# A decode step of attention plus a gated feed-forward: feed-forward moved behind head 0, and the output projection done by groups of heads

## Chip, cores and metric

One core of one Trainium2 chip. The metric is the device time of the slowest (here the only) core in microseconds (us), lower is better. The kernel before took 2587.42 us, the median of four runs (2586.26 to 2589.1). A single profile shows one execution; its span is about 1.8 us shorter than the time of that run.

## The reference

One token attends to a cache of 65536 positions with 32 heads. A feed-forward of the same token is mixed in by a scalar gate.

```python
# x (1,1,512) bf16; k_cache, v_cache (1,32,65536,128) bf16; wq (512,4096); wo (4096,512)
# w_gate, w_up (512,1792); w_down (1792,512); gate_w (512)
g = sigmoid((x * gate_w).sum(-1, keepdims=True))
q = (x @ wq) split into 32 heads of 128
p = softmax(q @ k_cache^T * 128 ** -0.5)
a = concat_heads(p @ v_cache) @ wo
b = (silu(x @ w_gate) * (x @ w_up)) @ w_down
out = g * a + (1 - g) * b
```

The two caches are 1074 MB together. Everything else that is read is about 16 MB.

## The kernel before

The DMA engines copy from the chip's memory (HBM) into its on-chip memory (SBUF); a transfer is asked for by an engine and stands in that engine's queue. K is read in tiles of 4 MB (two buffers) on SyncE's queue, V in tiles of 2 MB (three buffers) on ScalarE's. VectorE multiplies K by a broadcast q and folds the 128 products down to one score. ScalarE takes the exponential. TensorE multiplies V by the probabilities. Four chunks of 4096 positions make a segment (one K tile, two V tiles), and four segments a head.

```python
# ... q for all heads first: wq (4 MB) on nc.sync, 32 matmuls, 8 copies
with tc.tile_pool(name="ffn_w", bufs=1) as wpool:       # takes the room of wq, so it waits for q
    wg_sb = wpool.tile([P, KT, F], bf16, name="wg_sb");  nc.scalar.dma_start(out=wg_sb, in_=awg)
    wu_sb = wpool.tile([P, KT, F], bf16, name="wu_sb");  nc.sync.dma_start(out=wu_sb, in_=awu)
    # ... 112 small matmuls -> gu_ps, silu on VectorE, w_down on nc.scalar, 14 matmuls -> b_sb
wo_sb = _load_wo()                                        # nc.sync, takes the room of ffn_w
# ...
O_ps = psum_o.tile([P, H], f32, name="O_ps")
for h in range(H):
    for sgi, seg_chunks in enumerate(seg_plans[h]):
        for ci, c in enumerate(seg_chunks):
            # ... every 4th chunk: nc.sync.dma_start(out=K_big, in_=A_k_cache[...])
            nc.vector.tensor_tensor(out=prod, in0=K_t, in1=q_rep, op=ALU.mult)
            # ... four halving adds and a tensor_reduce -> S_sb
        nc.scalar.activation(out=P_sb, in_=S_sb, func=ACT.Exp, scale=scale, accum_out=rowsum[...])
        for ci, c in enumerate(seg_chunks):
            # ... every 2nd chunk: nc.scalar.dma_start(out=V_big, in_=A_v_cache[...])
            # ... 32 matmuls into O_ps[:, h : h + 1]
tot_ps = psum_tot.tile([P, H * NSEGMAX], f32, name="tot_ps")
nc.tensor.matmul(tot_ps, lhsT=ones, rhs=rowsum, start=True, stop=True)
tot_sb = consts.tile([P, H * NSEGMAX], f32, name="tot_sb")   # these three live among the constants
# ... tot_h = consts.tile([P, H]); recip = consts.tile([P, H]); oT = O_ps * recip
for h in range(H):
    nc.tensor.matmul(a_ps, lhsT=oT[:, h : h + 1], rhs=wo_sb[:, h, :], start=(h == 0), stop=(h == H - 1))
# ... out = (a - b) * g + b
```

The softmax here doesn't subtract the row's maximum and nothing guards it: scores larger than these inputs give would overflow.

Of the kernel before, what the change touches and what calls it, by code (L numbers as in the profile page):

```python
# [7 lines left out]
ACT = mybir.ActivationFunctionType  # L8
ALU = mybir.AluOpType
AXIS = mybir.AxisListType  # L10
P = 128
# [3 lines left out]
PROD_BUFS = 2  # L15
WMAX = 4096
CHUNKS_PER_SEG = 4
POOL_MULT_EVERY = 0
VQ = "scalar"
LAST_HEAD_SPLIT = 1  # L20
PROD_INPLACE = 0
DMA_MULT = 4
VDMA_MULT = 2
WQ_STAGED = 0
WO_LATE = 1
FFN_STAGED = 0
WO_ENG = "sync"
# [3 lines left out]
def kernel(  # L31
# [14 lines left out]
    nc = tc.nc  # L46
    bf16 = mybir.dt.bfloat16
    f32 = mybir.dt.float32

    _, H, Sk, Dh = A_k_cache.shape  # L50
    D = A_x.shape[2]
# [16 lines left out]

    consts = ctx.enter_context(tc.tile_pool(name="consts", bufs=1))
    psum_o = ctx.enter_context(tc.tile_pool(name="psum_o", bufs=1, space=bass.MemoryType.PSUM))  # L70
# [4 lines left out]

# [8 lines left out]
    gval = consts.tile([1, 1], f32, name="gval")  # L84

# [4 lines left out]
    def _load_wo():  # L90
        wo_pool = ctx.enter_context(tc.tile_pool(name="wo_pool", bufs=1))
        wo_sb = wo_pool.tile([P, H, D], bf16, name="wo_sb")
        {"gpsimd": nc.gpsimd, "sync": nc.sync, "scalar": nc.scalar}[WO_ENG].dma_start(
            out=wo_sb, in_=A_wo.rearrange("(h p) n -> p h n", p=P)
        )
        return wo_sb

    wo_sb = None
    if not WO_LATE:
        wo_sb = _load_wo()  # L100
# [3 lines left out]
    prodpool = None if PROD_INPLACE else ctx.enter_context(tc.tile_pool(name="prod", bufs=PROD_BUFS))  # L104
# [3 lines left out]
    awq = A_wq.rearrange("(t p) f -> p t f", p=P)  # L108
    with tc.tile_pool(name="wq_pool", bufs=(2 if WQ_STAGED else 1)) as wq_pool:
        if not WQ_STAGED:  # L110
            wq_sb = wq_pool.tile([P, KT, H * Dh], bf16, name="wq_sb")
            nc.sync.dma_start(out=wq_sb, in_=awq)
        for g in range(H // HG):
            if WQ_STAGED:
                wq_g = wq_pool.tile([P, KT, HG * Dh], bf16, name="wq_g")
                nc.sync.dma_start(out=wq_g, in_=awq[:, :, g * HG * Dh : (g + 1) * HG * Dh])
                w_rhs = lambda t: wq_g[:, t, :]
            else:
                w_rhs = lambda t: wq_sb[:, t, g * HG * Dh : (g + 1) * HG * Dh]
            qg_ps = psum_misc.tile([P, HG * Dh], f32, name="qg_ps", tag="misc")  # L120
            for t in range(KT):
                nc.tensor.matmul(  # L122
                    qg_ps,
                    lhsT=X_bc[:, t, :],
                    rhs=w_rhs(t),
                    start=(t == 0),
                    stop=(t == KT - 1),
                )
            nc.scalar.activation(  # L129
                out=q_bc_sb[:, g * HG * Dh : (g + 1) * HG * Dh], in_=qg_ps, func=ACT.Copy  # L130
            )

    awg = B_w_gate.rearrange("(t p) f -> p t f", p=P)
    awu = B_w_up.rearrange("(t p) f -> p t f", p=P)
    awd = B_w_down.rearrange("(t p) n -> p t n", p=P)
    GB = 4
    with tc.tile_pool(name="ffn_w", bufs=(2 if FFN_STAGED else 1)) as wpool:
        gu_ps = psum_misc.tile([P, 2 * FT], f32, name="gu_ps", tag="misc")
        if FFN_STAGED:
            for fb in range(0, FT, GB):  # L140
                nb = min(GB, FT - fb)
                for wi, aw in enumerate((awg, awu)):
                    w_b = wpool.tile([P, KT, GB * P], bf16, name="wgu_b")
                    nc.scalar.dma_start(
                        out=w_b[:, :, : nb * P], in_=aw[:, :, fb * P : (fb + nb) * P]
                    )
                    for fi in range(nb):
                        ft = fb + fi
                        for t in range(KT):
                            nc.tensor.matmul(  # L150
                                gu_ps[:, wi * FT + ft : wi * FT + ft + 1],
                                lhsT=w_b[:, t, fi * P : (fi + 1) * P],
                                rhs=xT[:, t : t + 1],
                                start=(t == 0),
                                stop=(t == KT - 1),
                            )
        else:
            wg_sb = wpool.tile([P, KT, F], bf16, name="wg_sb")
            nc.scalar.dma_start(out=wg_sb, in_=awg)
            wu_sb = wpool.tile([P, KT, F], bf16, name="wu_sb")  # L160
            nc.sync.dma_start(out=wu_sb, in_=awu)
# [10 lines left out]
        gu_sb = consts.tile([P, 2 * FT], f32, name="gu_sb")  # L172
        nc.vector.tensor_copy(out=gu_sb, in_=gu_ps)  # L173
        eg = consts.tile([P, FT], f32, name="eg")
        nc.scalar.activation(out=eg, in_=gu_sb[:, :FT], func=ACT.Exp, scale=-1.0)
        nc.vector.tensor_scalar_add(eg, eg, 1.0)
        nc.vector.reciprocal(eg, eg)
        hprod = consts.tile([P, FT], f32, name="hprod")
        nc.vector.tensor_tensor(out=hprod, in0=gu_sb[:, :FT], in1=eg, op=ALU.mult)
        hT = consts.tile([P, FT], bf16, name="hT")  # L180
        nc.vector.tensor_tensor(out=hT, in0=hprod, in1=gu_sb[:, FT:], op=ALU.mult)  # L181
        b_ps = psum_misc.tile([1, D], f32, name="b_ps", tag="misc")
        if not FFN_STAGED:
            wd_sb = wpool.tile([P, FT, D], bf16, name="wd_sb")
            nc.scalar.dma_start(out=wd_sb, in_=awd)
        for ft in range(FT):
            if FFN_STAGED:
                wd_b = wpool.tile([P, D], bf16, name="wd_b")
                nc.scalar.dma_start(out=wd_b, in_=awd[:, ft, :])
            else:  # L190
                wd_b = wd_sb[:, ft, :]
            nc.tensor.matmul(  # L192
                b_ps,
                lhsT=hT[:, ft : ft + 1],
                rhs=wd_b,
                start=(ft == 0),
                stop=(ft == FT - 1),
            )
        nc.vector.tensor_copy(out=b_sb, in_=b_ps)  # L199

        xg = consts.tile([1, D], f32, name="xg")
        s_t = consts.tile([1, 1], f32, name="s_t")
        nc.vector.tensor_tensor_reduce(
            out=xg, in0=x_row, in1=gw_row, scale=1.0, scalar=0.0,
            op0=ALU.mult, op1=ALU.add, accum_out=s_t,
        )
        eg2 = consts.tile([1, 1], f32, name="eg2")
        nc.scalar.activation(out=eg2, in_=s_t, func=ACT.Exp, scale=-1.0)
        nc.vector.tensor_scalar_add(eg2, eg2, 1.0)
        nc.vector.reciprocal(gval, eg2)  # L210

    if WO_LATE:
        wo_sb = _load_wo()
# [18 lines left out]
    O_ps = psum_o.tile([P, H], f32, name="O_ps")  # L232
    a_ps = psum_a.tile([1, D], f32, name="a_ps")
    oT = consts.tile([P, H], bf16, name="oT")

    chunk_counter = 0
    for h in range(H):
        qb = q_bc_sb[:, h * Dh : (h + 1) * Dh]
# [6 lines left out]
        for sgi, seg_chunks in enumerate(plan):  # L245
            segcols = len(seg_chunks) * J
            S_sb = spool.tile([P, SEGCOLS], f32, name="S_sb")
            for ci, c in enumerate(seg_chunks):
# [10 lines left out]
                prod = K_t if PROD_INPLACE else prodpool.tile([P, J, Dh], bf16, name="prod")  # L259
                mult_eng = nc.vector  # L260
                if POOL_MULT_EVERY and (chunk_counter % POOL_MULT_EVERY) == (POOL_MULT_EVERY - 1):
                    mult_eng = nc.gpsimd
                chunk_counter += 1
                mult_eng.tensor_tensor(out=prod, in0=K_t, in1=q_rep, op=ALU.mult)  # L264
# [15 lines left out]
            )  # L280
            for ci, c in enumerate(seg_chunks):
                m = c % VDMA_MULT
                if m == 0:
                    V_big = vpool.tile([P, VDMA_MULT * J, Dh], bf16, name="V_big")
                    veng = {"scalar": nc.scalar, "sync": nc.sync, "gpsimd": nc.gpsimd}[VQ] if VQ != "mix" else (nc.scalar if c % 2 == 0 else nc.gpsimd)
                    veng.dma_start(
# [6 lines left out]
                for j in range(J):  # L293
# [3 lines left out]
                        O_ps[:, h : h + 1],  # L297
# [4 lines left out]
                    )  # L302

    tot_ps = psum_tot.tile([P, H * NSEGMAX], f32, name="tot_ps")
    nc.tensor.matmul(tot_ps, lhsT=ones, rhs=rowsum, start=True, stop=True)  # L305
    tot_sb = consts.tile([P, H * NSEGMAX], f32, name="tot_sb")
    nc.vector.tensor_copy(out=tot_sb, in_=tot_ps)  # L307
    tot_h = consts.tile([P, H], f32, name="tot_h")
    if NSEGMAX > 1:
        nc.vector.tensor_reduce(  # L310
            out=tot_h, in_=tot_sb.rearrange("p (h s) -> p h s", s=NSEGMAX), axis=AXIS.X,
            op=ALU.add,
        )
    else:
        nc.vector.tensor_copy(out=tot_h, in_=tot_sb)
    recip = consts.tile([P, H], f32, name="recip")
    nc.vector.reciprocal(out=recip, in_=tot_h)
    nc.vector.tensor_tensor(out=oT, in0=O_ps, in1=recip, op=ALU.mult)  # L318

    for h in range(H):  # L320
        nc.tensor.matmul(  # L321
            a_ps,
            lhsT=oT[:, h : h + 1],
            rhs=wo_sb[:, h, :],
            start=(h == 0),
            stop=(h == H - 1),
        )
# [39 lines left out]
```

## Time and profile before

| what | value | where it is read |
|---|---|---|
| span of the profiled run | 2587.3 us (its time was 2589.1) | head of the page |
| DMA rate in the middle | 427 GB/s at a share of 1.00 to 1.01 | busy time by stretch |
| VectorE busy | 2471 us, 96% | page, part 1 |
| transfers nearly dry | 60 to 70 us | busy time by stretch |
| from the end of the last V product to the end of the span | 14.5 us | timeline |

The first fence is from the page of the kernel before: the span, the busy times, the DMA share in 40 slices (in tenths), the rate in each slice, and the chain of work that ended last.

```profile
span 2587.3 us, 37728 instructions
...
PE 500.9 (19%) x16576; PEld 468.0 (18%) x16576; DVE 2471.0 (96%) x3093; ACT 58.9 (2%) x273; POOL 0.4 (0%) x5
...
DMA  9999999999999999999999999999999999999996
GB/s 377 377 423 429 429 429 428 428 429 430 428 427 427 429 422 430 429 424 426 431 426 428 425 428 425 432 427 424 429 425 427 426 429 427 424 430 425 426 426 289
...
DMA V_big<-in_A_v_cache_dram 73%; DVE prod L268 8%; DVE prod L264 8%; PE O_ps L296 5%; DMA K_big<-in_A_k_cache_dram 1%; DVE S_sb L272 1%; DMA wq_sb<-in_A_wq_dram 1%; DMA wg_sb<-in_B_w_gate_dram 1%; PE qg_ps L122 0%; PE a_ps L321 0%; PE gu_ps L165 0%; PE tot_ps L305 0%; DVE out_sb L332 0%; DVE diff L330 0%; DVE b_sb L199 0%
```

The DMA engines are full from end to end; only the first two slices and the last are slow. The Trainium skill, "DMA: Bandwidth & Descriptors", Specifications, gives 435 GB/s as the ceiling of the fabric; the middle of this trace sits 2% below it. The next fence is the view of busy time by stretch of the same kernel. In each row come the length of the stretch, busy us and instruction count of each engine, then TensorE's clock, DMA share and GB/s.

```profile
core 0: us, PE busy (x) PEld busy (x) DVE busy (x) ACT busy (x) POOL busy (x), PEclk, DMA share, GB/s
...
60.00:65.00 5.00, 2.43 (x92) 2.35 (x88) 2.53 (x8) 0.22 (x1) 0.00 (x0) 0.50 0.67 211
65.00:70.00 5.00, 0.00 (x0) 0.00 (x0) 5.00 (x5) 0.00 (x0) 0.00 (x0) 0.50 0.15 39
...
1100.00:1600.00 500.00, 95.19 (x3264) 91.01 (x3264) 492.05 (x613) 10.46 (x52) 0.00 (x0) 0.50 1.01 427
1600.00:2100.00 500.00, 95.17 (x3264) 91.00 (x3264) 490.00 (x612) 10.06 (x50) 0.00 (x0) 0.50 1.00 427
```

The timeline of the same kernel says why they ran dry. Its columns are start, length, engine and line, and in brackets the idle time before with what ended it.

```profile
36.99 0.37 SPq L161 DMA_DIRECT2D wu_sb<-in_B_w_up_dram  x1
...
37.40 31.82 SPq L252 DMA_DIRECT2D K_big<-in_A_k_cache_dram  x2
...
43.62 3.56 DVE L268 TENSOR_TENSOR prod<-prod 128x2048 bf16<-128x2048 bf16 x4
...
62.47 0.19 DVE L173 COPY gu_sb<-gu_ps 128x28 f32<-128x28 f32 x1 [15.29 <-PE gu_ps L165]
...
2570.94 1.87 PE L296 MATMUL O_ps<-P_sb,V_big 128*128 128x1 bf16 x64 [2.99 <-DMA V_big<-in_A_v_cache_dram]
2572.64 0.50 PEld L305 LDWEIGHTS tot_ps<-rowsum,ones 128*128 128x128 f32 x2
2572.66 1.09 PE L305 MATMUL tot_ps<-rowsum,ones 128*128 128x224 f32 x2
...
2575.28 8.38 PE L321 MATMUL a_ps<-wo_sb,oT 128*1 128x512 bf16 x32 [1.52 <-DVE oT L318]
...
2585.18 0.26 SPq L336 DMA_DIRECT2D out_dram<-out_sb  x1
```

VectorE stopped for 15.3 us in the middle of the first K tile, because its copy of the feed-forward product stands there in its order. The third K tile could not be asked for until VectorE was done with the first (the second of the two K issues on that line ends at 69 us). At the end, 32 projection matmuls of 8.4 us stand between the last V product and the output.

### The profile page before, as it was taken

What the parts mean: (1) busy time and instruction counts of PE and PEld (TensorE: products, weight loads), DVE (VectorE), ACT (ScalarE), POOL (GpSimd) and SP (SyncE); (2) the same over time, 40 slices, a digit from 0 to 9 for tenths busy, and PEclk for the clock granted to TensorE, in tenths of its full rate; (3) what the DMA queues carried; (4) which work ended last, traced back from release to release, by engine and by line L of the source; (5) the groups of instructions that cost most, each with busy time, mean ns of one, the idle gap of its engine ahead of it and who ended that gap; (6) DMA issues with size and microseconds to landing.
All of it is one profiled execution on the core that took longest, in us unless ns stands there. A gap on an engine that the chain in (4) does not pass through costs nothing.

```text
span 2587.3 us, 37728 instructions
## 1 busy us (share of the span) xinstructions
PE 500.9 (19%) x16576; PEld 468.0 (18%) x16576; DVE 2471.0 (96%) x3093; ACT 58.9 (2%) x273; POOL 0.4 (0%) x5
## 2 busy tenths in 40 slices
PE   1211211211111212111212211121221112122113
PEld 1111211111111111111111111111111111111112
DVE  1899999999999999999999999999999999999996
ACT  1000000000000000000000000000000000000000
POOL 0000000000000000000000000000000000000000
PEclk8555555555555555555555555555555555555555
DMA  9999999999999999999999999999999999999996
GB/s 377 377 423 429 429 429 428 428 429 430 428 427 427 429 422 430 429 424 426 431 426 428 425 428 425 432 427 424 429 425 427 426 429 427 424 430 425 426 426 289
DMA packets 63498, 1090.06 MB, mean 421 GB/s; under 512 B 6755, under 2 KB 12646, under 8 KB 13670
## 3 DMA queue, kind: packets, MB, share of 16 engines
q1 hardware_dynamic: 24134, 547.11, 49.7%
q10 hardware_dynamic: 39200, 540.56, 49.3%
q8 instruction: 129, 2.11, 0.3%
q14 instruction: 35, 0.29, 0.0%
HBM read 1087.64 MB, written 0.00 MB: 420 GB/s over the span
## 4 chain that ended last, share of the span: by engine, by line
DMA 76%; DVE 17%; PE 6%; issue 0%; SPq 0%; ACT 0%; DVEq 0%; ACTq 0%
DMA V_big<-in_A_v_cache_dram 73%; DVE prod L268 8%; DVE prod L264 8%; PE O_ps L296 5%; DMA K_big<-in_A_k_cache_dram 1%; DVE S_sb L272 1%; DMA wq_sb<-in_A_wq_dram 1%; DMA wg_sb<-in_B_w_gate_dram 1%; PE qg_ps L122 0%; PE a_ps L321 0%; PE gu_ps L165 0%; PE tot_ps L305 0%; DVE out_sb L332 0%; DVE diff L330 0%; DVE b_sb L199 0%
## 5 line engine op out<-in xcount | busy, mean ns | idle before, releaser
L264 DVE TENSOR_TENSOR prod<-K_big,q_bc_sb 128x4096 bf16<-128x4096 bf16 x512 | 1148.4, 2284 | 67.3 <-DMA K_big<-in_A_k_cache_dram 66.5
L268 DVE TENSOR_TENSOR prod<-prod 128x2048 bf16<-128x2048 bf16 (+3 forms) x2048 | 1186.0, 651 | 0.0
L296 PE MATMUL O_ps<-P_sb,V_big 128*128 128x1 bf16 x16384 | 474.4, 165 | 2021.6 <-DMA V_big<-in_A_v_cache_dram 1667.4
L296 PEld LDWEIGHTS <-V_big 128*128 128x128 bf16 x16384 | 456.6, 104 | 2039.7 <-DMA V_big<-in_A_v_cache_dram 1796.3
L272 DVE TENSOR_REDUCE S_sb<-prod 128x32 f32<-128x256 bf16 x512 | 188.9, 410 | 0.5 <-DVE prod L268 0.5
L277 ACT ACTIVATE P_sb<-S_sb 128x128 bf16<-128x128 f32 (+1 forms) x131 | 40.2, 307 | 2452.2 <-PE O_ps L296 1527.2
L277 ACT ACTIVATION_READ_ACCUMULATOR P_sb<-S_sb 128x1 f32 x131 | 24.4, 186 | 0.0
L173 DVE COPY gu_sb<-gu_ps 128x28 f32<-128x28 f32 x1 | 0.2, 187 | 15.3 <-PE gu_ps L165 15.3
L122 PE MATMUL qg_ps<-wq_sb,X_bc 128*128 128x512 bf16 x32 | 8.7, 441 | 28.2 <-DMA wq_sb<-in_A_wq_dram 28.2
L307 DVE COPY tot_sb<-tot_ps 128x224 f32<-128x224 f32 x1 | 0.4, 392 | 12.9 <-PE tot_ps L305 12.9
L122 PEld LDWEIGHTS <-X_bc 128*128 128x128 bf16 x32 | 3.5, 110 | 33.0 <-issue 20.7
L330 DVE TENSOR_TENSOR diff<-a_ps,b_sb 1x512 f32<-1x512 f32 x1 | 0.7, 679 | 8.5 <-PE a_ps L321 8.5
L321 PE MATMUL a_ps<-wo_sb,oT 128*1 128x512 bf16 x32 | 8.4, 428 | 1.5 <-DVE oT L318 1.5
L88 DVE COPY X_bc<-xT 128x128 bf16<-128x128 bf16 x4 | 0.6, 220 | 8.3 <-DMA xT<-in_A_x_dram 8.3
L165 PE MATMUL gu_ps<-xT,wg_sb 128*128 128x1 bf16 x56 | 3.0, 165 | 22.3 <-DMA wg_sb<-in_B_w_gate_dram 22.3
L192 PE MATMUL b_ps<-wd_sb,hT 128*1 128x512 bf16 x14 | 5.4, 568 | 9.0 <-DVE hT L181 9.0
L165 PEld LDWEIGHTS <-wg_sb 128*128 128x128 bf16 x56 | 2.6, 104 | 22.8 <-issue 22.8
L129 ACT ACTIVATE q_bc_sb<-qg_ps 128x512 bf16<-128x512 f32 x8 | 4.8, 597 | 21.9 <-PE qg_ps L122 21.9
L321 PEld LDWEIGHTS <-oT 128*1 128x1 bf16 x32 | 2.9, 92 | 7.1 <-DVE oT L318 2.1
L192 PEld LDWEIGHTS <-hT 128*1 128x1 bf16 x14 | 1.5, 114 | 12.5 <-DVE hT L181 9.1
L165 PE MATMUL gu_ps<-xT,wu_sb 128*128 128x1 bf16 x56 | 3.0, 165 | 0.0
L165 PEld LDWEIGHTS <-wu_sb 128*128 128x128 bf16 x56 | 2.6, 104 | 0.0
(24 smaller groups left out, 8.3 us busy)
## 6 DMA issues: line engine op xcount, KB each, us to landing
V_big<-in_A_v_cache_dram ACTq DMA_DIRECT2D x256, 2048.0 KB, 25.5
K_big<-in_A_k_cache_dram SPq DMA_DIRECT2D x128, 4096.0 KB, 19.8
wq_sb<-in_A_wq_dram SPq DMA_DIRECT2D x1, 4096.0 KB, 26.3
wo_sb<-in_A_wo_dram SPq DMA_DIRECT2D x1, 4096.0 KB, 37.1
wu_sb<-in_B_w_up_dram SPq DMA_DIRECT2D x1, 1792.0 KB
wg_sb<-in_B_w_gate_dram ACTq DMA_DIRECT2D x1, 1792.0 KB, 22.1
wd_sb<-in_B_w_down_dram ACTq DMA_DIRECT2D x1, 1792.0 KB
xT<-in_A_x_dram SPq DMA_DIRECT2D x1, 1.0 KB, 8.7
```

The costliest lines, as they stand in the source:

```text
L88: nc.vector.tensor_copy(out=X_bc[:, t, :], in_=xT[:, t : t + 1].to_broadcast([P, P]))
L122: nc.tensor.matmul(qg_ps, lhsT=X_bc[:, t, :], rhs=w_rhs(t), start=(t == 0), stop=(t == KT - 1),)
L129: nc.scalar.activation(out=q_bc_sb[:, g * HG * Dh : (g + 1) * HG * Dh], in_=qg_ps, func=ACT.Copy)
L165: nc.tensor.matmul(gu_ps[:, wi * FT + ft : wi * FT + ft + 1], lhsT=wsb[:, t, ft * P : (ft + 1) * P], rhs=xT[:, t : t + 1], start=(t == 0), ...
L192: nc.tensor.matmul(b_ps, lhsT=hT[:, ft : ft + 1], rhs=wd_b, start=(ft == 0), stop=(ft == FT - 1),)
L264: mult_eng.tensor_tensor(out=prod, in0=K_t, in1=q_rep, op=ALU.mult)
L268: nc.vector.tensor_tensor(out=prod[:, :, 0:half], in0=prod[:, :, 0:half], in1=prod[:, :, half : 2 * half], op=ALU.add,)
L272: nc.vector.tensor_reduce(out=S_sb[:, ci * J : (ci + 1) * J], in_=prod[:, :, 0:8], axis=AXIS.X, op=ALU.add,)
L277: nc.scalar.activation(out=P_sb[:, :segcols], in_=S_sb[:, :segcols], func=ACT.Exp, scale=scale, accum_out=rowsum[:, h * NSEGMAX + sgi : h ...
L296: nc.tensor.matmul(O_ps[:, h : h + 1], lhsT=V_t[:, j, :], rhs=P_sb[:, col : col + 1], start=(gcol == 0), stop=(gcol == NB - 1),)
L321: nc.tensor.matmul(a_ps, lhsT=oT[:, h : h + 1], rhs=wo_sb[:, h, :], start=(h == 0), stop=(h == H - 1),)
L330: nc.vector.tensor_tensor(out=diff, in0=a_ps, in1=b_sb, op=ALU.subtract)
```

## The change

Two things are intended. The feed-forward and wo are put behind head 0 in program order, with wo on GpSimd's queue, so that K and V stream from the start. The normalisation and projection of finished heads are done inside the stream, in groups of 8, 8, 8 and 7 heads, so that only head 31 is left for the end. Selectors that were always off are removed as well.

```diff
-WO_ENG = "sync"
+WO_ENG = "gpsimd"
+FFN_POS = 0
...
-    psum_o = ctx.enter_context(tc.tile_pool(name="psum_o", bufs=1, space=bass.MemoryType.PSUM))
+    psum_o = ctx.enter_context(tc.tile_pool(name="psum_o", bufs=2, space=bass.MemoryType.PSUM))
...   (feed-forward and wo load become functions; w_down is now asked for with the other two)
+    groups = [list(range(g, min(g + 8, H - 1))) for g in range(0, H - 1, 8)] + [[H - 1]]
+    def _project(heads, O_g):
+        n, lo = len(heads), heads[0]
+        tot_ps = psum_tot.tile([P, 8 * NSEGMAX], f32, name="tot_ps")
+        nc.tensor.matmul(tot_ps[:, : n * NSEGMAX], lhsT=ones, rhs=rowsum[...], start=True, stop=True)
+        tot_h = spool.tile([P, 8], f32, name="tot_h")
+        ...   (tensor_reduce, reciprocal, product -> oT[:, lo : lo + n])
+        for h in heads:
+            nc.tensor.matmul(a_ps, lhsT=oT[:, h : h + 1], rhs=wo_holder["wo"][:, h, :], ...)
...
     for h in range(H):
+        if h == group[0]:
+            O_ps = psum_o.tile([P, 8], f32, name="O_ps")
...   (after the exponential of a segment)
+            if due and sgi == 1:
+                _project(*due)
+                due = None
...   (after the V products of a head)
+        if h == group[-1]:
+            due = (group, O_ps)
+        if h == FFN_POS:
+            _compute_ffn()
+            _load_wo()
-    tot_sb = consts.tile([P, H * NSEGMAX], f32, name="tot_sb")
-    tot_h = consts.tile([P, H], f32, name="tot_h")
-    recip = consts.tile([P, H], f32, name="recip")
-    ...   (the old tail)
+    _project(*due)
```

Keep the last three removed allocations in mind: 896 + 128 + 128 = 1152 bytes per partition (one of the 128 rows of SBUF) leave the constants, and the K, V, product and score tiles, which are allocated behind them, move down by as much.

## The prediction

> **What bounds the kernel now.** The DMA engines. The 40 slices show them at 9 tenths or more in all but the last; the stretches from 100 to 2520 us move 427 to 428 GB/s. The Trainium skill, "DMA: Bandwidth & Descriptors", Specifications, gives 435 GB/s as the fabric ceiling; the trace sits 2% under it. VectorE is nearly as full (busy 2471 of 2587 us); in those 2420 us it waited for K about 38 us, so it could run only 1.6% faster than the transfers. The chain of waits: V transfers 73%, VectorE 17%. Both kernels move 1090 MB, 2547 us at 428 GB/s, so only about 40 us are open, at the two ends.
>
> **What the change does, costed from the trace of before.**
> 1. Start. K tile 1 was queued behind the up-weights, which wait for q (issue at 37.0 us); V tiles 1 and 2 sat behind the gate's exponential until 10.7 us. Then VectorE stopped from 47.2 to 62.5 us for the feed-forward's first product (15.3 us wait), which held K tile 2 back to 69 us, and the transfers ran dry: 211 GB/s in 60 to 65 us, 39 in 65 to 70. Afterwards K tile 1 is queued directly behind K tile 0, three V tiles go out at the start, and VectorE's feed-forward comes after head 0. VectorE still starts at about 39 us, then runs on without the 15.3 us wait and most of the 12.9 us wait for K at 113 us. But what counts is transfer time: summed bytes show the transfers 16 us behind a 428 GB/s line at 200 us; 4 are the start, about 3 the short rows of w_down and wo; the other 9 to 10 us come back.
> 2. End. After the last V product (2572.8 us) the old tail runs the total (1.0 us), four small VectorE instructions and 32 projection matmuls, 8.4 us, until 2583.7. Afterwards only head 31 is left: a short total, three small instructions, one matmul; an estimate of 1.5 us from the single durations. Gain 9 to 9.5 us.
> 3. Added in the stream: four projections. VectorE about 0.5 us each, plus a wait for TensorE's total, which stands behind the last V product of the previous group; before, VectorE was one to two segments ahead of that: an estimate of 0 to 10 us each. TensorE does 8 matmuls of about 0.4 us in its idle time (19% busy). Queued transfers should hide most of this.
> 4. wo moves to GpSimd's queue, at about 130 us. The Trainium skill, "SBUF — State Buffer", Who interferes with whom, warns that descriptor writing there can be shut out by some VectorE modes, but not, as it infers, by tensor_tensor. Not needed before 650 us, so no cost even if slow.
>
> **Predicted:** 2568 us, range 2560 to 2577. Faster by over 2%: 0.02; within 2%: 0.97; slower: 0.01.
>
> **Shown right by:** no dip of GB/s at 60 to 70 us; no VectorE wait for the feed-forward, and short waits for K in mid-stream instead; 427 to 428 GB/s in the middle; about 5 us between the last V product and the end, against 14.5.
>
> **Wrong if:** the projections stall VectorE long enough to empty the transfer queues (dips near 650, 1280, 1900, 2480 us); wo on GpSimd's queue slows the other transfers; or the middle was held by VectorE, when the earlier VectorE start would give up to 28 us instead of 10.

## The result, and the profile after

The changed kernel took 2575.64 us, median of nine runs (2575.43 to 2576.53); the kernel before 2587.15 us over 13 runs (2582.39 to 2590.66). The ratio is 0.9956, with a 95% interval of 0.9947 to 0.9966. Ratios here are the mean time of one kernel's fast runs over that of the other's of the same rounds, so not quite the ratio of the medians quoted. The change is thus worth 11.5 us, where 19 were expected. All outputs are right.

From the page of the changed kernel:

```profile
span 2573.8 us, 37749 instructions
...
PE 511.7 (20%) x16584; PEld 470.8 (18%) x16584; DVE 2473.2 (96%) x3104; ACT 58.6 (2%) x273; POOL 2.2 (0%) x6
...
DMA  9999999999999999999999999999999999999998
GB/s 402 423 418 424 428 427 430 429 427 427 429 425 427 425 429 425 423 430 423 427 427 428 424 428 424 425 430 427 425 429 422 429 427 426 424 426 428 426 427 342
...
DMA V_big<-in_A_v_cache_dram 89%; PE O_ps L305 6%; DVE prod L275 1%; DMA K_big<-in_A_k_cache_dram 1%; DVE prod L271 1%; DVE S_sb L279 0%; DVE out_sb L323 0%; DVE diff L321 0%; PE a_ps L238 0%; PE tot_ps L222 0%; SPq L76 0%; SPq L126 0%; SPq L78 0%; ACT P_sb L284 0%; SPq L80 0%
```

Busy time by stretch of the changed kernel:

```profile
60.00:65.00 5.00, 3.24 (x121) 3.16 (x119) 5.00 (x5) 0.00 (x0) 0.00 (x0) 0.50 1.02 429
65.00:70.00 5.00, 0.97 (x37) 0.91 (x35) 5.00 (x10) 0.00 (x0) 0.00 (x0) 0.50 0.91 324
...
1100.00:1600.00 500.00, 99.22 (x3274) 92.29 (x3274) 489.77 (x615) 10.05 (x50) 0.00 (x0) 0.50 1.00 426
1600.00:2100.00 500.00, 96.88 (x3210) 90.46 (x3210) 488.87 (x609) 10.05 (x50) 0.00 (x0) 0.50 1.00 426
```

The end in the timeline of the changed kernel:

```profile
2560.51 1.87 PE L305 MATMUL O_ps<-P_sb,V_big 128*128 128x1 bf16 x64 [2.98 <-DMA V_big<-in_A_v_cache_dram]
...
2566.78 1.86 PE L305 MATMUL O_ps<-P_sb,V_big 128*128 128x1 bf16 x64 [4.40 <-DMA V_big<-in_A_v_cache_dram]
2568.50 0.57 PE L222 MATMUL tot_ps<-rowsum,ones 128*128 128x7 f32 x2
...
2569.72 0.59 PE L238 MATMUL a_ps<-wo_sb,oT 128*1 128x512 bf16 x1 [0.65 <-DVE oT L234]
...
2571.83 0.26 SPq L327 DMA_DIRECT2D out_dram<-out_sb  x1
```

What VectorE waited for in the changed kernel (total us, times, longest):

```profile
DVE prod L271 <- DMA K_big<-in_A_k_cache_dram: 38.1, 56, 5.1
DVE tot_h L227 <- PE tot_ps L222: 23.4, 5, 11.1
```

The hole at 60 to 70 us is filled (the DMA share is 1.02 and 0.91; the 324 GB/s fall in the time when, by the packet records, the 1 KB rows of w_down move), the tail is 5.2 us from the end of the last V product (2573.8 less 2568.64), and the four projections in the stream hold VectorE for about 3 us each (23.4 less the 11.1 at the very end, over four). All of that is as expected. But the middle runs at 426 GB/s and not 427, over 2000 us. One digit is too coarse, so a finer measure is used from here on: the **lag**, which is the time at some point less the bytes moved by then divided by 428 GB/s, with the bytes summed from the rates of stretches of 10 us. Where it grows, transfer time is being lost.

| lag, us, at | 100 | 300 | 700 | 2500 | growth 700 to 2500 |
|---|---|---|---|---|---|
| before | 15.3 | 15.6 | 15.1 | 19.1 | 4.0 |
| changed | 4.3 | 6.4 | 6.4 | 14.1 | 7.7 |

So 9 us of head start at 300 us were 5 us at 2500.

### The profile page after: what moved, and what is told of

It reads as the page before. It is cut to its first block, busy times and chain, and to the rows that moved or that the text cites. A ratio compares the mean times of both kernels' runs of the same rounds, so it can differ in the third digit from the quotient of the medians.

```text
span 2573.8 us, 37749 instructions
## 1 busy us (share of the span) xinstructions
PE 511.7 (20%) x16584; PEld 470.8 (18%) x16584; DVE 2473.2 (96%) x3104; ACT 58.6 (2%) x273; POOL 2.2 (0%) x6
## 4 chain that ended last, share of the span: by engine, by line
DMA 90%; PE 6%; DVE 3%; issue 0%; SPq 0%; ACT 0%
DMA V_big<-in_A_v_cache_dram 89%; PE O_ps L305 6%; DVE prod L275 1%; DMA K_big<-in_A_k_cache_dram 1%; DVE prod L271 1%; DVE S_sb L279 0%; DVE out_sb L323 0%; DVE diff L321 0%; PE a_ps L238 0%; PE tot_ps L222 0%; SPq L76 0%; SPq L126 0%; SPq L78 0%; ACT P_sb L284 0%; SPq L80 0%
## 5 line engine op out<-in xcount | busy, mean ns | idle before, releaser
L275 DVE TENSOR_TENSOR prod<-prod 128x2048 bf16<-128x2048 bf16 (+3 forms) x2048 | 1215.1, 650 | 0.0
L271 DVE TENSOR_TENSOR prod<-K_big,q_bc_sb 128x4096 bf16<-128x4096 bf16 x512 | 1158.5, 2284 | 40.8 <-DMA K_big<-in_A_k_cache_dram 38.1
L279 DVE TENSOR_REDUCE S_sb<-prod 128x32 f32<-128x256 bf16 x512 | 199.0, 410 | 0.0
L227 DVE TENSOR_REDUCE tot_h<-tot_ps 128x8 f32<-128x56 f32 (+2 forms) x5 | 1.0, 205 | 23.4 <-PE tot_ps L222 23.4
L238 PE MATMUL a_ps<-wo_sb,oT 128*1 128x512 bf16 x32 | 13.8, 603 | 0.6 <-DVE oT L234 0.6
```

The lines of the kernel that those rows point to most:

```text
L227: nc.vector.tensor_reduce(out=tot_h[:, :n], in_=tot_ps[:, : n * NSEGMAX].rearrange("p (h s) -> p h s", s=NSEGMAX), axis=AXIS.X, op=ALU.add,)
L238: nc.tensor.matmul(a_ps, lhsT=oT[:, h : h + 1], rhs=wo_holder["wo"][:, h, :], start=(h == 0), stop=(h == H - 1),)
L275: nc.vector.tensor_tensor(out=prod[:, :, 0:half], in0=prod[:, :, 0:half], in1=prod[:, :, half : 2 * half], op=ALU.add,)
L279: nc.vector.tensor_reduce(out=S_sb[:, ci * J : (ci + 1) * J], in_=prod[:, :, 0:8], axis=AXIS.X, op=ALU.add,)
```

## The experiments

Two theories were stated first. **A**: the projections inside the stream cost transfer time. **B**: they are free, but a VectorE that starts earlier reaches sooner a state in which each K issue waits for a V landing (SyncE waited for V 96 times in the kernel before and 119 times in the changed one, by the view of waits), and in that state a little bandwidth is lost. The lags of all profiles are gathered in one table after the runs.

### Control, and the two halves

The changed kernel again on the chip that ran the halves:

> Control: the changed kernel unaltered, on the same chip as the two halves. Both theories: about 11.5 us below the kernel before (2575 to 2577 us).

Measured: 2575.68 us against 2586.82; as expected.

Only the end:

```diff
-WO_ENG = "gpsimd"
+WO_ENG = "sync"
-FFN_POS = 0
+FFN_POS = -1      # feed-forward and wo in front of the heads again
```

> Only the end of the change: projections by groups of eight heads, with the feed-forward, wo and their queues where the kernel before has them. The tail after the last V product shrinks from 14.5 to about 5.1 us in any case. Theory A (the four projections inside the stream cost transfer time, about 5 us in all): 4 to 6 us faster than before. Theory B (the projections are free; the 5 us go because an earlier VectorE reaches sooner the state in which K transfers wait for V landings): 9 to 9.5 us faster than before, with the transfers' lag behind 428 GB/s at 2500 us the same as in before (about 19 us).

Measured: 2581.89 us, 4.9 faster than before (ratio 0.9969 to 0.9996). Its tail is the short one, yet its lag at 2500 us is 20.3.

Only the start:

```diff
-    groups = [list(range(g, min(g + 8, H - 1))) for g in range(0, H - 1, 8)] + [[H - 1]]
+    groups = [list(range(H))]      # and tiles [P, 8] -> [P, H]: one projection, at the end
```

> Only the start of the change: feed-forward after head 0, wo on GpSimd's queue, but all 32 heads projected at the end as in before. Theory A: the full 9 to 9.5 us of the start come through to the end (lag at 2500 us about 9 to 10 us). Theory B: only 4 to 6 us faster than before, as the lag grows from about 6 us at 600 us to 14 us at 2500 us, as in the changed kernel.

Measured: 2584.45 us, 2.4 faster than before. By its interval (ratio 0.9979 to 1.0004) that is not clear of noise, though all five runs lie below all nine of the kernel before. Its lag is 6.7 at 700 us and 14.0 at 2500, though nothing is projected in its stream.

Both theories fall here. A said that the start alone would keep its 9 us; it lost 7.3 us between 700 and 2500 without any projection in the stream. B said that the end alone would lose nothing more than before, because its VectorE starts no earlier; it lost 7.5 us between 700 and 2500 and came out 4.9 us faster, not 9 (the lag that B named for 2500 us, about 19, is near the 20.3 measured, but this run began from 12.5). The two halves sum to 7.3 us and the whole is worth 11.1, as if each half paid the same price once.

### wo on SyncE's queue

```diff
-WO_ENG = "gpsimd"
+WO_ENG = "sync"
```

> The changed kernel with wo on SyncE's queue in place of GpSimd's. If GpSimd's queue costs the other transfers something (lag 4.6 us at 140 us, 6.7 us at 230 us, about 2 us in all), this gains up to 2 us; if the lag is the price of the 1 KB rows, whoever issues them, it is the same within 1 us; if wo now holds K tiles back in SyncE's order, it loses a few us.

Measured: 2577.98 us, 2.3 slower than the changed kernel beside it. The lag jumps from 5.5 at 150 us to 9.4 at 300, and VectorE waits 21.3 us once for K, since K tiles now stand behind wo in SyncE's order. So GpSimd's queue was the better place. Lines from the page of the changed kernel, from the page of this run, and from this run's busy time by stretch:

```profile
DMA packets 60426, 1090.06 MB, mean 424 GB/s; under 512 B 6755, under 2 KB 8550, under 8 KB 10598
...
q0 software_dynamic: 1040, 4.19, 0.4%
```

```profile
DMA packets 63498, 1090.06 MB, mean 423 GB/s; under 512 B 6755, under 2 KB 12646, under 8 KB 13670
```

```profile
190.00:200.00 10.00, 1.52 (x58) 1.52 (x58) 10.00 (x13) 0.40 (x2) 0.00 (x0) 0.50 0.83 327
```

Two things show. On SyncE's queue wo went as 4096 packets of 1 KB, which took 13.0 us of each engine's time (12.8 in the kernel before); on GpSimd's it went as 1024 packets of 4 KB, 10.4 us. And the engines ran partly dry for 10 us (share 0.83). No run separates the two. The Trainium skill, "SBUF — State Buffer", Who interferes with whom, warns that descriptor writing on GpSimd can be shut out by some VectorE modes but tells of a probe in which two-input operations (tensor_tensor) did not do it, and infers why; here, under such products, the issue took 1.8 us and the landing 100 us (37 in the kernel before), 500 us ahead of need. No engine waited for it. Whether the long landing is descriptor writing that was held up, or the sharing with K and V, the trace does not show.

### Is the profile of before a lucky one?

The kernel before, against itself:

> Control: the kernel before against itself, on one chip. The ratio should be 1.000 within 0.1%. The question is its profile: does a second profile of it also lose only about 4 us between 700 and 2500 us (lag behind a 428 GB/s line), where all four profiles of kernels built from the changed one lost 7 to 7.5? If it loses about 7 as well, the difference in the middle was the luck of one profile, and the head start of about 9 us should show in the medians; if it loses 4 again, the middle is really better in the kernel before.

Measured: 2587.23 against 2587.19 us, ratio 1.0000 (0.9987 to 1.0012). Two things follow. The growth from 700 to 2500 us is 3.8 again, so the middle of the kernel before really is better. And its lag at 300 us is 13.0 in this profile, 15.6 in the first: the start differs from run to run by more than 2 us, and one profile had overstated what there was to win.

### Deeper and finer queues

Four V buffers in the changed kernel (a scratch row is shared to make room):

```diff
-VT_BUFS = 3
+VT_BUFS = 4
-    diff = consts.tile([1, D], f32, name="diff")
+    diff = xg
```

> The changed kernel with four V buffers in place of three (one scratch row shared to make room). Theory B (the middle loses because few transfers are outstanding once VectorE runs ahead and each K issue waits for a V landing): the loss between 700 and 2500 us falls from 7 us to under 4, the dip near the end (about 350 GB/s for three us) goes too, in all 3 to 5 us faster than the changed kernel (2571 to 2573 us). Theory C (the DMA engines move no more than about 427 GB/s of this traffic, waits or not): within 1 us of 2575.7 but for about 1 us at the end.

Measured: 2575.49 us, 0.2 from the changed kernel. The growth fell only to 5.5, and what was won was lost again after 2550 us. Theory B's 3 to 5 us did not come.

The same edit in the kernel before:

> The kernel before with four V buffers. Theory B: little in the middle (it lost only 4 us there), about 1 us at the end: 2583 to 2586 us. Theory C: the same within 1 us but for the end.

Measured: 2582.39 us, 4.8 faster than before and a little more than expected, mostly at the start (lag 8.8 at 300 us). Growth in the middle: 1.9.

K in tiles of half the size:

```diff
-KT_BUFS = 2
+KT_BUFS = 4
-DMA_MULT = 4
+DMA_MULT = 2
```

> The changed kernel with K in four tiles of 2 MB in place of two of 4 MB, in the same room. Theory B: K is asked for in smaller and earlier pieces, so more is outstanding: the loss between 700 and 2500 us falls by 2 to 4 us. Theory C: the same within 1 us. The start could change by a few us either way, as the order on SyncE's queue puts the up-weights behind eight K tiles instead of two.

Measured: 2586.26 us, 10.6 slower than the changed kernel; growth 10.5. Theory B was wrong in sign here. This run has K rows of 16 KB in place of 32 KB, so more rows for the same bytes, and that pointed at the cost of a row (its row times follow below).

### A third theory: the place

Queue depth moved the loss little, and neither half had escaped it. What all kernels built from the changed one share is where their tiles lie. In the built programs the first K tile starts at byte 37984 of each partition before, which is 96 past a multiple of 256, and at 36832 after, which is 224 past one. The difference is the 896 + 128 + 128 = 1152 bytes per partition (one of the 128 rows of SBUF) that left the constants with the last three removed allocations. The V tiles have the same remainders. The trace's packet records show one packet for each row of K (32 KB) and of V (16 KB), and its time follows the place. Quartiles and means over 1200 to 2400 us from the span's start, in ns, computed from these records (no view prints them):

| first byte of K and V, past a multiple of 256 | V row: quartiles, mean | K row: quartiles, mean |
|---|---|---|
| 96 (before) | 611, 612, 615; 615.4 | 1213, 1214, 1218; 1229.5 |
| 224 (changed) | 612, 614, 614; 616.6 | 1214, 1216, 1216; 1229.5 |

The mean of K hangs on the slowest 3% of its rows and moves by about 1 ns with the stretch taken, so it does not tell the two apart; the other columns do.

**Theory D**: the place of the tiles sets the time of each row. **Rival E**: the rows take longer because of the changed order of work. The edits only add unused bytes in front of the constants, and everything behind moves up by as much.

```diff
+    pad = consts.tile([P, BYTES // 4], f32, name="pad")   # 32, 1152, 128 or 416 bytes
+    nc.gpsimd.memset(pad, 0.0)
     ones = consts.tile([P, P], f32, name="ones")
```

The changed kernel, 32 bytes, so that K and V start on multiples of 512:

> The changed kernel with 32 unused bytes in front of its constants, so that every K and V tile starts on a multiple of 512 bytes (before: 96 past a multiple of 256; changed: 224 past). Theory D (where the tiles lie in SBUF sets the time of each row's transfer: in ten profiles the median 16 KB row of V takes 612 ns in the kernel before and 614 in the changed one, and the difference of means times 32768 V rows and 16384 K rows over 16 engines is about 3 us): V rows at 612 ns or less, K rows at 1214 or less, and 3 us or more faster than the changed kernel: 2572.5 us or less. Rival E (the packets take longer because of the changed order of work, not the place): 614 ns as before and 2575.7 us within 1 us.

Measured: 2558.57 us (four runs, 2558.42 to 2558.91), ratio to before 0.9887 (0.9874 to 0.9901). That is 17 us faster than the changed kernel and far more than expected. V rows took 611 ns in all three quartiles and K rows 1213. From its page, and from its busy time by stretch:

```profile
span 2557.1 us, 37750 instructions
...
GB/s 404 425 424 429 429 430 434 429 432 430 435 426 430 426 431 429 429 434 423 434 426 429 434 425 427 429 430 430 424 432 427 429 431 430 429 423 429 430 431 343
```

```profile
1100.00:1600.00 500.00, 98.91 (x3274) 92.22 (x3274) 492.38 (x619) 10.46 (x52) 0.00 (x0) 0.50 1.00 429
1600.00:2100.00 500.00, 99.17 (x3274) 92.24 (x3274) 490.87 (x614) 10.07 (x50) 0.00 (x0) 0.50 1.00 429
```

The middle moves 429 GB/s with the same instructions in the same order, where the changed kernel moved 426.

The changed kernel, 1152 bytes, so that it lies where the kernel before lay:

> The changed kernel with 1152 unused bytes in front, so that its K, V, product and score tiles lie exactly at the addresses of the kernel before. Theory D: V rows back at 612 ns, the loss between 700 and 2500 us falls from 7.5 to about 4 us, 2571.5 to 2573 us. Rival E: 614 ns, 2575.7 us within 1 us.

Measured: 2571.41 us, 4.3 faster than the changed kernel; V rows at 611, 612, 615, the very quartiles of before; growth 5.0.

The kernel before, 128 bytes, which gives it the remainder of the changed one:

> The kernel before with 128 unused bytes in front: its K and V tiles then stand 224 bytes past a multiple of 256, as in the changed kernel. Theory D: V rows at 614 ns, the loss in the middle grows from 4 to about 7.5 us, 2590 to 2591 us. Rival E: 612 ns and 2587.2 us within 1 us.

Measured: 2592.95 us, ratio 1.0018 (1.0004 to 1.0032); V rows at 613, 614, 614; growth 6.4. The time is 2 us beyond what was expected; this profile also had a late start (lag 16.6 at 300 us).

The kernel before, 416 bytes, aligned:

> The kernel before with 416 unused bytes in front, so that every K and V tile starts on a multiple of 512 bytes: the last corner of a table of two orders of work and three places. Theory D with place and order adding up: rows at 611 and 1213 ns, and 16 to 17 us slower than the changed kernel at aligned places, as at the other two places: 2574.5 to 2576 us. If at aligned places VectorE became the limit of the middle, the changed order's earlier VectorE start would be worth more, and this run would lie at 2580 us or above.

Measured: 2572.91 us, ratio 0.9943 (0.9929 to 0.9957); rows at 611 and 1213 ns. It is 14.3 us slower than the changed kernel at aligned places, slightly less than the 16 to 17 expected, and VectorE did not become a new limit.

Theory D stands on both sides: the same order of work changes speed with its place, and two orders at the same place show the same row times. Rival E is refuted. Which tile's place counts is not shown: K, V, product and score tiles move together in every run.

| medians, us | before's order | changed order | the change is worth |
|---|---|---|---|
| 96 past a multiple of 256 | 2587.2 | 2571.4 | 15.8 |
| 224 past | 2593.0 | 2575.7 | 17.3 |
| on a multiple of 512 | 2572.9 | 2558.6 | 14.3 |

The kernels as given are the top left and the middle right: 11.5 us apart.

How far do the row times account for it? An estimate from the packet records: 16 engines share 32768 V rows and 16384 K rows, so each moves 2048 and 1024. With the mean times of that stretch, 616.6 and 1229.5 ns (changed) against 613.1 and 1224.3 (aligned), that is 7.2 + 5.3 = 12.5 us of the 17.1. Against 615.5 and 1228.5 ns (changed order at before's place) it is 2.3 + 1.0 = 3.3 of the 4.3. For the unsteady mean of K, these sums are good to about 1 us. The other 4 to 5 us of the aligned run are not accounted for; the padding moves every tile, not K and V alone (VectorE's product went from 2284 to 2280 ns, for one).

The same estimate fits the run with K tiles of half the size, which lies where the changed kernel lies. Two of its 16 KB rows of K took 1237.5 ns together, where one row of 32 KB took 1229.5, and its V rows took 617.7 ns against 616.6: 8.2 + 2.3 = 10.5 of the 10.6 us. So the place is not all that sets a row's time.

The Trainium skill, "DMA: Bandwidth & Descriptors", How a descriptor splits into AXI transactions, says that when a descriptor (one piece of a transfer) does not start on a multiple of 256 bytes, its first transaction starts at the multiple below, and the bytes in front are fetched and not used. The runs agree in direction, with 611, 612 and 614 ns for a 16 KB row at 0, 96 and 224 past. They do not show that this is the mechanism: the page counts the bytes of reads, while here the source in HBM was the same and the place in SBUF differed.

### The lags of all profiles

| profile | 300 us | 700 us | 2500 us | growth 700 to 2500 | past 256 |
|---|---|---|---|---|---|
| before, twice | 15.6, 13.0 | 15.1, 12.5 | 19.1, 16.3 | 4.0, 3.8 | 96 |
| changed, twice | 6.4, 6.3 | 6.4, 6.9 | 14.1, 14.3 | 7.7, 7.4 | 224 |
| end only | 12.5 | 12.8 | 20.3 | 7.5 | 224 |
| start only | 6.6 | 6.7 | 14.0 | 7.3 | 224 |
| changed, wo on SyncE | 9.4 | 9.1 | 16.6 | 7.5 | 224 |
| changed, four V buffers | 6.4 | 6.5 | 12.0 | 5.5 | 224 |
| before, four V buffers | 8.8 | 8.1 | 10.0 | 1.9 | 96 |
| changed, K tiles of 2 MB | 7.8 | 9.5 | 20.0 | 10.5 | 224 |
| changed, aligned | 4.3 | 1.7 | -2.1 | -3.8 | 0 |
| changed, at before's place | 6.2 | 6.0 | 11.0 | 5.0 | 96 |
| before, shifted | 16.6 | 16.6 | 23.0 | 6.4 | 224 |
| before, aligned | 12.6 | 10.0 | 6.0 | -4.0 | 0 |

With three V buffers and 4 MB K tiles the growth goes with the last column: about 4 to 5 at 96, 6.4 to 7.7 at 224, about -4 at 0. A negative number only means that the rate is above the 428 of the line.

## Why the prediction was right or wrong

The measured 2575.6 us lies inside the predicted 2560 to 2577, and "within 2%" was right. The point, 2568, was 7.6 us too low. That the range held was partly luck: the prediction did not know that the tiles would move, and at the three places tried the same order of work took 2558.6, 2571.4 and 2575.7 us, the first of them outside the range.

- **The limit: right.** The DMA engines held the middle in all runs, and an earlier VectorE did not speed it up.
- **Start: right mechanism, mis-sized.** The hole at 60 to 70 us went, VectorE began at 38.6 us, and the lag at 300 us is 6.4 as expected. "The other 9 to 10 us come back" was read from one profile with a late start. By the second profile of the kernel before the gain is 6.7 us (13.0 less 6.3), and about 2.4 of that can be the larger packets of wo on GpSimd's queue (12.8 less 10.4 us of each engine's time), which the prediction did not have.
- **End: right.** From the end of the last V product to the end of the span it is 5.2 us instead of 14.5, a gain of 9.3. In the second profile of before the same 32 matmuls took 9.25 us in place of 8.38, so it can be a us more.
- **Projections in the stream: right.** VectorE waited about 3 us each, within the 0 to 10 expected, and the growth of the lag is the same with them (7.7, 7.4) and without (7.3).
- **wo on GpSimd's queue: right as to harmless,** and better than that: SyncE's queue costs 2.3 us in the changed kernel.
- **"427 to 428 GB/s in the middle": wrong, and this is the step that failed.** The prediction took the rate of the middle as given. The change had moved all tiles down by 1152 bytes, the V rows took 0.2% longer (616.6 against 615.4 ns on the mean; of K only the median rose, from 1214 to 1216), and the growth of the lag rose from about 4 to 7.5 us. Putting the tiles back gave 4.3 us.

The sum from the two later profiles of the two kernels: at 300 us 6.7 us ahead; 4.7 lost by 2500 us (the lag of before grew by 3.3 from 300 us on, that of the changed kernel by 8.0), most of it the place; about 1 lost in the last V tiles; 10.2 won from the start of the last V product to the end. That makes about 11, the difference of their spans (2585.1 and 2574.1).

Left open: why the start of the old order varies between 12.5 and 16.6 us of lag; and why the last V tile of the kernels with both the grouped projection and wo on GpSimd's queue lands late (4.2 to 4.5 us of waiting before the last V product, against 3.0 in the kernel before and in both halves), about 1.4 us.

## What to carry to other kernels

In a kernel bound by transfers, look up where the big tiles start in SBUF after every edit: an edit far away can move them, and 32 unused bytes were worth about as much here (17 us) as the whole reordering (14 to 17 us). When two halves of a change add up to less than the whole, look for a cost that each pays once, such as the layout they share. When a fraction of a per cent is at stake, profile the baseline twice before sizing a gain from it.

## What the Trainium skill lacked or had wrong

- "DMA: Bandwidth & Descriptors", How a descriptor splits into AXI transactions, counts what an unaligned start costs in reads. It lacks the time by the place in SBUF that a load writes to: with the same source, a 16 KB row took 611, 612 and 614 ns (medians) at 0, 96 and 224 bytes past a multiple of 256, and a 1 GB stream 2558.6, 2571.4 and 2575.7 us.
- "SBUF — State Buffer", Operand start alignment, says of itself that it is about legality and timed nothing. All starts here were legal; the two unaligned ones cost 0.5% and 0.7%.
- "SBUF — State Buffer", the summary of rules, says to use about 358 GB/s for loads from HBM, and the row does not say that this is a core's share when its neighbour streams too (other pages of the skill do). This core alone held 426 to 429 GB/s for two milliseconds, near the 435 of the fabric that the DMA page has.
- The same summary advises against GpSimd's queue for a load under VectorE work, because of VectorE's faster modes. Here wo (4 MB) on GpSimd's queue was 2.3 us better than on SyncE's, where it went in packets of 1 KB and not 4 KB and the K tiles queued behind it; its landing took 100 us, which did not matter.
